# Scores in groups over six shared PSUM banks, in a fused block-sparse attention and MLP kernel

## The chip, the cores and the metric

The kernel runs on one core of a Trainium2 chip. The metric is device time in microseconds: the median of several executions. TensorE (PE) multiplies and writes its results to PSUM; VectorE (DVE) and ScalarE (ACT) read PSUM, compute and write to SBUF; GpSimd (POOL) issues most loads; SyncE (SP) issues transposing DMAs and stores. The engines run side by side, each its own instructions in order, and wait for each other by semaphores.

## The reference

```python
scores = (1/8) * q @ k.T                  # 4 batches, 8 heads, 768 tokens, 64 per head
mask   = |blk_i - blk_j| <= 1, first and last block row and column, and three sampled
         blocks for each of the 24 blocks of 32 tokens
attn   = softmax(where(mask, scores, -1e9))
x      = attn @ v                         # heads side by side: (4, 768, 512)
a1     = alpha1 * x + beta1
u      = x + lam * (w_tok @ a1)           # over tokens, w_tok 768 x 768
a2     = alpha2 * u + beta2
out    = u + lam * (relu(a2 @ w_ch1) @ w_ch2)     # 512 -> 2048 -> 512
```

## The kernel before

**The work.** Two heads of one batch are a pair; there are 16 pairs. The scores of a pair, keys on the partitions, are cut into 9 units of 1024 columns, 144 units in all. A unit goes through TensorE (scores), ScalarE (exponential, to a tile eT in f16), for pairs 6 to 15 VectorE (minimum with a mask tile, L760), and TensorE again (product with v). In pairs 0 to 5 ("single") the mask is folded into the score product by 24 more rows (88 rows, L651). In pairs 6 to 15 ("paired") the two heads lie on the two halves of the partitions, 64 rows each, and their score products run side by side in two row tiles of TensorE (L729). 90 units are paired ones.

**The lines that the text names.** On TensorE: L170 warming, L218 transposes of q and k, L228 the block mask, L651 and L729 scores, L691 and L787 products with v into the tile ops, L864 the token product, L946 the first channel product (four matmuls of 384 columns each, 128 times), L997 the second (groups of four matmuls of 512 columns into the tile cp or ops). On ScalarE: L666 and L755 exponentials, L959 relu of L946 into hts, L278 and L280 (VectorE) copies, among them that of the column b1t, which the first half of the first batch has beside each relu. On VectorE: L963 the same relu, L623 and L626 the normalisation of ops, L844 and L852 the input of the token product, L874 its sum into x_sb, L880 the input of the channel product, L456 scaling of w2b, L1014 the last sum ahead of a store (L1021). On SP: L590 transposes q and k of a paired pair, L911 transposes u. POOL loads at L316.

**The order.** It is not written out by hand. `Job` objects hold an engine, a length, a priority, dependencies and the buffers that they take and give. A loop at the end of the function plays the jobs by their lengths over the engines and emits each one when its engine is free, its inputs are there and its buffers can be had. `pin_order` then fixes this order on each engine. What the planner believes thus decides the order of instructions; the semaphores decide when they run.

**PSUM.** There are eight banks of 512 columns. Before, they are tiles of fixed kinds: two score buffers `sps` of two banks each, two buffers `mm` of one bank for transposes, token products and the first channel product, one `cp` and one `ops`. In `paired`, units are put in groups of two, and a group takes both `sps` at once:

```python
jq = Job("PE", 2 * 225.0 + 175.0, (1, i0), qk, deps, take=("sps", "sps"), give=give)
```

The 225 and 175 ns are the planner's lengths of a unit and of a visit to the scores. The channel product may take an `sps` only once no scores are left. `LEAD` (15 units) limits how far the scores of the later pairs may run ahead of the channel products. Each tile's dependencies are drawn by the framework, by tile.

Of the kernel before, what the change touches and what calls it, by code (L numbers as in the profile page):

```python
# [39 lines left out]
LEAD = 15  # L40
# [9 lines left out]
def pin_order(nc, tc):  # L50

    last = {}
    for ins in list(nc.cur_bb.bb.instructions):
        prev = last.get(ins.engine)
        if prev is not None:
            tc.add_manual_dep(
                ins,
                prev,
                mybir.DependencyInfo(
                    mybir.DependencyClass.NoSync, mybir.DependencyReason.DATA  # L60
                ),
                reason="program order",
            )
        last[ins.engine] = ins.name


@with_exitstack
def kernel(
# [78 lines left out]
    def mm_tile(shape, dt=FP):  # L147
        return ps.tile(shape, dt, name="mm", tag="mm", bufs=2)
# [66 lines left out]
    def transposes(rel, a, slots=range(NT)):  # L215
        tps = mm_tile([P, NT, P], BF)
        for o in slots:
            nc.tensor.transpose(tps[:, o, :], rel[:, a, o, :], identb[:])  # L218
        return tps[:].rearrange("p o c -> p (o c)")
# [3 lines left out]
    flatA = transposes(rel0, 0, range(0, 3))  # L223
    flatB = transposes(rel0, 0, range(3, 6))
    bqs = []
    for w, tag in ((0, "sps"), (1, "ops")):
        t = ps.tile([P, UN if tag == "sps" else 512], FP, name=tag, tag=tag, bufs=2 if tag == "sps" else 1)
        nc.tensor.matmul(  # L228
            t[0:NBLK, 0:HS], mbb[MB, :], kx[0][MB, ts(w, HS)], start=True, stop=True
        )  # L230
        bqs.append(t)
# [7 lines left out]
    for j in range(2, NQB):  # L239
# [14 lines left out]
        sps=2, mm=2, cp=1, ops=1, eT=NET, head=NQB, vext=NV, ld=NLD, rel=3,  # L254
# [5 lines left out]
    class Job:  # L260
        def __init__(self, eng, dur, prio, fn, deps=(), take=(), give=(), lat=None):
            self.eng = eng if isinstance(eng, tuple) else (eng,)
            self.dur, self.prio, self.fn = dur, prio, fn
            self.deps = list(deps)
            self.take, self.give = take, give
            self.lat = lat
            self.alt = {}
            self.xfer = None
            self.late = 0.0
            self.bulk = None  # L270
            self.done = None
            self.gate = None
            self.n = len(jobs)
            jobs.append(self)
# [146 lines left out]
    for t in range(NT):  # L421

        def tr(t=t):
            tl["wt", t] = tp = mm_tile([P, NT, P], BF)
            for s in range(NT):
                nc.tensor.transpose(tp[:, s, :], wtk_tile[0][:, t, s : S : NT], identb[:])

        def cp_(eng, t=t):
            copy(eng, wtokT[:, :, ts(t, P)], tl.pop(("wt", t))[:])

        j = Job("PE", mmt(NT, P), (5, t), tr, [wload["tok", t // 2]], take=("mm",))
        last = t == NT - 1
        wtok_jobs.append(
            Copy((4, t), cp_, [j], give=("mm", "w2b") if last else ("mm",), only=False)
        )
# [83 lines left out]
    for p in range(len(pairs)):  # L519
        if p == 0:  # L520
# [4 lines left out]
            def f_tr():  # L525
                tl["h0"] = transposes(rel0, 1)
# [9 lines left out]
            j = Job("PE", mmt(NT, P), (2, 0), f_tr, [j], take=("mm",))  # L536
            j = Copy((1, 0, 1), f_cq, [j, head_ready[0]], take=("head",), only=3 >= 0)
            j = Copy((1, 0, 2), f_ck, [j], give=("mm", "rel"), only=3 >= 0)
# [6 lines left out]
        elif p < NPE:  # L545
# [12 lines left out]
            for a in range(2):  # L558
                h = 2 * p + a

                def tr(p=p, a=a, h=h):
                    tl["hd", h] = transposes(rels[p], a)
# [7 lines left out]
                jt = Job("PE", mmt(NT, P), (2, p, a), tr, [ck, prev], take=("mm", "head"),  # L570
# [3 lines left out]
                prev = head_ready[h] = Job("NONE", 0.0, (0,), lambda: None, [j1, j2], give=("mm",), lat=0.0)  # L574
# [37 lines left out]
    grp = []  # L612
    exps = []
# [22 lines left out]
    def single(p):  # L636
# [3 lines left out]
        for u in range(NU):  # L640
            i = p * NU + u

            def qk(p=p, u=u):
                sps = ps.tile([P, UN], FP, name="sps", tag="sps", bufs=2)
# [29 lines left out]
            jq = Job("PE", mmt(2, 512) + (8 if u % 3 != 1 else 8), (1, i), qk, deps, take=("sps",), give=give)  # L674
            jq.gate = i
            qk_jobs[i] = jq
            exp_jobs[i] = je = Job("ACT", 950.0, (1, i), ex, [jq], take=("eT",), give=("sps",), lat=160.0)
# [35 lines left out]
    def paired(p):  # L713
        nonlocal last_pv
        b, n = pairs[p]
        mins = []
        for u in range(NU):
            i = p * NU + u
            grp.append((p, u))
            if len(grp) == 2:  # L720

                def qk(units_=tuple(grp)):
                    for pp_, u_ in units_:
                        sps = ps.tile([P, UN], FP, name="sps", tag="sps", bufs=2)
                        sl = slot_of(pp_)
                        for lo, jt, c, w in pieces(u_):
                            for a in range(2):
                                r = slice(a * D, (a + 1) * D)
                                nc.tensor.matmul(  # L729
                                    sps[:, a * 512 + lo : a * 512 + lo + w],  # L730
                                    kx[sl][r, ts(jt, P)],
                                    qx[sl][r, c : c + w],
                                    start=True,
                                    stop=True,
                                )
                        tl["sps", pp_, u_] = sps
                        st["qk"] += 1

                give = sum((("head",) for _, u_ in grp if u_ == NU - 1), ())
                deps = [head_ready[2 * pp_] for pp_, _ in grp]  # L740
                i0 = grp[0][0] * NU + grp[0][1]
                deps.append(qk_jobs[i0 - 1])
                jq = Job("PE", 2 * 225.0 + 175.0, (1, i0), qk, deps, take=("sps", "sps"), give=give)
                jq.gate = i
                for pp_, u_ in grp:
                    qk_jobs[pp_ * NU + u_] = jq
                grp.clear()

        for u in range(NU):
# [14 lines left out]
            exps.append((p, u, ex, mn))  # L764

        while exps and (exps[0][0] * NU + exps[0][1]) in qk_jobs:
            p_, u, ex, mn = exps.pop(0)
            i = p_ * NU + u
            je = Job("ACT", 950.0, (1, i), ex, [qk_jobs[i]], take=("eT",), give=("sps",), lat=160.0)
            min_jobs[i] = Job("DVE", 690.0, (1, i), mn, [je] + mask_jobs)  # L770
            if u == NU - 1:
                pv_of(p_)
# [55 lines left out]
    for p in range(len(pairs)):  # L828
# [29 lines left out]
        for g in range(2):  # L858

            def tok(p=p, g=g):  # L860
                tl["tp", p, g] = tp = mm_tile([P, 3, P])
# [10 lines left out]
            def xadd(p=p, g=g, n=n, s0=s0):  # L872
                sl = x_sb[:, s0 + 3 * g : s0 + 3 * g + 3, 2 * n * D : (2 * n + 2) * D]
                nc.vector.tensor_tensor(out=sl, in0=sl, in1=tl.pop(("tp", p, g))[:], op=ALU.add)  # L874
# [10 lines left out]
            jt = Job("PE", mmt(18, P), (3, p, g), tok, a_jobs + wtok_jobs, take=("mm",),  # L885
                     give=("a1p",) if g else ())
            jx = Job("DVE", 555.0, (1, p, g), xadd, [jt], give=("mm",))
# [8 lines left out]
        if b == 0:  # L896

            def utr(p=p):
                tl["up", p] = up = mm_tile([P, NT, P], BF)
# [3 lines left out]
            def ucp(eng, p=p, n=n, ut_tile=ut_tile):  # L903
                copy(eng, ut_tile()[:, n, 0:S], tl.pop(("up", p))[:].rearrange("p o c -> p (o c)"))

            j = Job("PE", mmt(NT, P), (2, p, 9), utr, ubs, take=("mm",), give=("ub",))
            ut_jobs[p] = Copy((1, p, 9), ucp, [j], take=take, give=("mm",))
# [22 lines left out]
    for kk in range(2 * B):  # L930
# [4 lines left out]
        for f in range(16):  # L935

            def c1(kk=kk, b=b, hf=hf, f=f, nc_=nc_):
                if f == 0:
                    hts[kk] = wk.tile([P, 16, HS], BF, name="hts", tag="hts", bufs=2)
                if tl.pop(("mmsel", kk, f)) == "sps":  # L940
                    hp = ps.tile([P, UN], FP, name="sps", tag="sps", bufs=2)
                else:
                    hp = mm_tile([P, 512])
# [31 lines left out]
            take = ((("mm", "sps"), ("mmsel", kk, f)),) + (("hts",) if f == 0 else ())  # L975
# [11 lines left out]
        for mi, (m, lo, w) in enumerate(parts):  # L987
            prev = last_m
            for r in range(4):

                def c2(kk=kk, m=m, r=r, mi=mi, lo=lo, w=w):
                    if r == 0:
                        tag = tl.pop(("cpsel", kk, mi))
                        shape = [P, UN] if tag == "sps" else [P, DM]
                        cps[kk, mi] = ps.tile(shape, FP, name=tag, tag=tag, bufs=2 if tag == "sps" else 1)
# [10 lines left out]
                take = ((("cp", "ops", "sps") if kk == 2 * B - 1 else ("cp", "ops"), ("cpsel", kk, mi)),) if r == 0 else ()  # L1006
# [33 lines left out]
    def can(j):  # L1040
        for t in j.take:
            if isinstance(t, tuple):
                opts = t[0]
                ok = False
                for o in opts:
                    if o == "sps" and not attention_over():
                        continue
# [4 lines left out]
                    if slots[o] > 0:  # L1052
# [9 lines left out]
    def gated(j):  # L1062
        return j.gate is not None and j.gate >= NS and j.gate - NS > st["ch"] / rate + LEAD

# [21 lines left out]
    while left:  # L1086
        moved = True
        while moved:
            moved = False
            for e in free_at:  # L1090
# [3 lines left out]
                if e == "POOL" and dma_free[0] - t > AHEAD:  # L1094
                    seq += 1
                    heapq.heappush(events, (dma_free[0] - AHEAD, -seq, None))
                    continue
                for r, j in by_eng[e]:
# [5 lines left out]
                    if (best is None or key < best[0]) and can(j):  # L1104
                        best = (key, j)
                if best is None:
# [3 lines left out]
                for tk in j.take:  # L1110
                    if isinstance(tk, tuple):
                        o = chosen[tk[1]]
                        slots[o] -= 1
# [31 lines left out]
                heapq.heappush(events, (j.done, seq, j))  # L1145
                if e == "PE":
# [9 lines left out]
                left -= 1  # L1156
# [6 lines left out]
        while events and events[0][0] <= t:  # L1163
# [7 lines left out]
            for g in j.give:  # L1171
                if isinstance(g, tuple):
                    slots[tl.pop(("slot", g))] += 1
                else:
                    slots[g] += 1
            for s in succ.get(j.n, ()):
# [3 lines left out]
                if not waiting[s.n]:  # L1180
                    for e in s.eng:
                        by_eng[e].append((t, s))
    pin_order(nc, tc)
# [30 lines left out]
```

## Time and profile before

| | us |
|---|---|
| median of 5 runs | 315.52 |
| lowest, highest | 315.1, 316.17 |
| the profiled execution, own time | 315.66 |
| its span, first to last instruction | 313.9 |
| busy: TensorE, VectorE, ScalarE | 305.5, 213.4, 198.1 |

The profile is of one execution. Busy time is the sum over an engine's instructions; the chain follows the work that ended last backwards, from each instruction to what released it. The timeline lists instructions by start. Ends of matmuls are modelled and overlap with the next start, so the pace of TensorE is read from start to start.

### The profile page before, as it was taken

How to read it: one execution, taken by the hardware profiler on the slowest of the kernel's cores; microseconds unless marked ns; L12 is line 12 of the kernel's file. 1: busy time of each engine (PE TensorE's matmuls, PEld its weight loads, DVE VectorE, ACT ScalarE, POOL GpSimd, SP SyncE). 2: the span in 40 equal slices, each digit the busy share in tenths (PEclk: the TensorE clock that was granted, in tenths of full speed). 3: DMA queues.
4: the chain of work that ended last, by engine and by line, in shares of the span. 5: the costliest groups of instructions: out<-in, count | busy, mean ns of one | idle time of the engine just before them, and what ended most of it. 6: DMA issues, size and time to landing. Idle time of an engine off the chain costs nothing.

```text
span 313.9 us, 7579 instructions
## 1 busy us (share of the span) xinstructions
PE 305.5 (97%) x3197; PEld 187.2 (60%) x3197; DVE 213.4 (68%) x447; ACT 198.1 (63%) x259; POOL 52.1 (17%) x91
## 2 busy tenths in 40 slices
PE   7999999988999999999999999999999999999995
PEld 3687888764646655565646655565656565555444
DVE  4599988859888687788869787788859671010111
ACT  4999988985778664766587654766587502828000
POOL 4646332000211220220310220230000000000000
PEclk9999999999999999999999999999999999999999
DMA  6999999994354555626462655626010203010021
GB/s 151 184 237 220 213 202 212 175 113 95 39 96 78 76 111 105 115 55 108 85 103 26 111 110 109 111 40 121 37 28 4 56 36 92 0 69 0 35 101 67
DMA packets 47210, 30.81 MB, mean 98 GB/s; under 512 B 27552, under 2 KB 43080, under 8 KB 47176
## 3 DMA queue, kind: packets, MB, share of 16 engines
q0 software_dynamic: 15984, 15.47, 31.9%
q1 hardware_dynamic: 30940, 14.61, 19.8%
q8 instruction: 25, 0.41, 0.7%
q10 hardware_dynamic: 252, 0.24, 0.3%
q14 instruction: 9, 0.07, 0.1%
HBM read 32.04 MB, written 6.33 MB: 122 GB/s over the span
## 4 chain that ended last, share of the span: by engine, by line
PE 80%; DMA 12%; issue 3%; DVE 2%; ACT 1%; POOL 1%; POOLq 0%
PE mm L946 23%; PE cp L997 22%; PE ops L787 8%; PE sps L729 7%; PE mm L864 7%; DMA v<-in_v_dram 6%; PE ops L997 5%; DMA k<-in_k_dram 4%; PE sps L946 2%; PE sps L651 2%; DMA q<-in_q_dram 2%; PE cp L170 2%; PE ops L691 1%; PE mm L218 1%; DVE ot L1014 1%
## 5 line engine op out<-in xcount | busy, mean ns | idle before, releaser
L755 ACT ACTIVATE eT<-sps 128x1024 f16<-128x1024 f32 x90 | 88.3, 1020 | 31.1 <-PE sps L729 28.8
L946 PE MATMUL mm<-uT,w1b 128*128 128x384 bf16 (+1 forms) x468 | 88.8, 326 | 2.7 <-DVE x_sb L874 2.2
L959 ACT ACTIVATE hts<-mm,b1t 128x384 bf16<-128x384 f32 x82 | 47.7, 582 | 49.3 <-PE mm L946 47.2
L997 PE MATMUL cp<-w2b,hts 128*128 128x512 bf16 (+1 forms) x320 | 76.9, 374 | 0.2
L946 PEld LDWEIGHTS <-w1b 128*128 128x128 bf16 x512 | 46.3, 97 | 34.7 <-issue 6.2
L760 DVE TENSOR_TENSOR eT<-eT,maskT 128x1024 f16<-128x1024 f16 x90 | 60.5, 684 | 4.1 <-ACT eT L755 4.0
L997 PEld LDWEIGHTS <-hts 128*128 128x128 bf16 x400 | 36.8, 97 | 35.7 <-issue 2.1
L666 ACT ACTIVATE eT<-sps 128x1024 f16<-128x1024 f32 (+1 forms) x55 | 52.1, 1024 | 3.1 <-PE sps L651 2.8
L787 PEld LDWEIGHTS <-eT 128*128 128x128 f16 x720 | 29.9, 97 | 15.9 <-issue 5.6
L1014 DVE TENSOR_TENSOR ot<-x_sb,cp 128x512 f32<-128x512 f32 (+1 forms) x20 | 13.4, 671 | 37.0 <-PE cp L997 36.8
L864 PE MATMUL mm<-a1p,wtokT 128*128 128x128 bf16 x576 | 36.2, 219 | 0.0
L787 PE MATMUL ops<-vext,eT 128*128 128x65 f16 x720 | 35.4, 193 | 0.0
L864 PEld LDWEIGHTS <-wtokT 128*128 128x128 bf16 x576 | 33.0, 98 | 2.1 <-issue 0.4
L651 PE MATMUL sps<-qx,kx 88*128 88x512 bf16 (+1 forms) x144 | 31.6, 325 | 0.6 <-ACT qx L237 0.5
L314 POOL COPY held<-flag 1x1 bf16<-1x1 bf16 x24 | 9.2, 384 | 130.7 <-DVE flag L334 130.7
L963 DVE TENSOR_SCALAR hts<-mm,b1t 128x384 bf16<-128x384 f32 x35 | 21.5, 616 | 13.5 <-PE mm L946 13.2
L729 PE MATMUL sps<-qx,kx 64*128 64x512 bf16 (+1 forms) x240 | 27.3, 326 | 0.0
L874 DVE TENSOR_TENSOR x_sb<-x_sb,mm 128x384 f32<-128x384 f32 x32 | 17.6, 550 | 4.7 <-PE mm L864 4.3
L691 PEld LDWEIGHTS <-eT 128*128 128x128 f16 x432 | 18.2, 97 | 4.4 <-DVE x_sb L626 0.6
L691 PE MATMUL ops<-vext,eT 128*128 128x65 f16 x432 | 20.2, 193 | 0.0
L626 DVE TENSOR_TENSOR x_sb<-ops,rcp 128x384 f32<-128x384 f32 x32 | 17.8, 557 | 1.1
L729 PEld LDWEIGHTS <-kx 64*128 64x128 bf16 x240 | 8.0, 94 | 16.5 <-issue 14.1
(71 smaller groups left out, 237.0 us busy)
## 6 DMA issues: line engine op xcount, KB each, us to landing
out_dram<-ot SPq DMA_DIRECT2D x23, 256.0 KB
v<-in_v_dram POOLq DMA_DIRECT2D x16, 192.0 KB, 5.5
q<-in_q_dram POOLq DMA_DIRECT2D x15, 192.0 KB, 4.1
k<-in_k_dram POOLq DMA_DIRECT2D x15, 192.0 KB, 4.4
w1b<-in_moe_w_ch_dram POOLq DMA_DIRECT2D x4, 512.0 KB, 9.9
w2b<-in_moe_w_ch_dram POOLq DMA_DIRECT2D x4, 512.0 KB, 15.9
wtk<-in_moe_w_tok_dram POOLq DMA_DIRECT2D x3, 384.0 KB, 9.5
maskT<-mask_rows SPq DMA_DIRECT2D x14, 72.0 KB
```

The costliest lines, as they stand in the source:

```text
L651: nc.tensor.matmul(sps[:, f - u * UN : f - u * UN + w], kx[h][0:KC, ts(jt, P)], qx[h][0:KC, c : c + w], start=True, stop=True,)
L666: nc.scalar.activation(eT[:, c], sps[:, c], AF.Exp, bias=EXPB, scale=SCALE)
L691: nc.tensor.matmul(ops[p, a][:, t * VW : t * VW + D + 1], eTs[p, u][:, ts(i - u * GU, P)], vx[:, a, jt, 0 : D + 1], start=(i % HT == 0), s ...
L729: nc.tensor.matmul(sps[:, a * 512 + lo : a * 512 + lo + w], kx[sl][r, ts(jt, P)], qx[sl][r, c : c + w], start=True, stop=True,)
L755: nc.scalar.activation(eT[:], sps[:], AF.Exp, bias=EXPB, scale=SCALE)
L760: nc.vector.tensor_tensor(out=e, in0=e, in1=maskT[:, u, :].unsqueeze(1).broadcast_to([P, 2, 512]), op=ALU.min,)
L787: nc.tensor.matmul(ops[p, a][:, t * VW : t * VW + D + 1], eTs[p, u][:, a * 512 + c * P : a * 512 + (c + 1) * P], vx[:, a, jt, 0 : D + 1], ...
L864: nc.tensor.matmul(tp[:, j, :], wtokT[:, s, ts(3 * g + j, P)], tl["a1p", p][:, s, :], start=(s == 0), stop=(s == NT - 1),)
L946: nc.tensor.matmul(hp[:, 0:nc_], w1b[:, dk, ts(f, P)], uTs[b][:, dk, hf * HS : hf * HS + nc_], start=(dk == 0), stop=(dk == 3),)
L959: nc.scalar.activation(hts[kk][:, f, :], hp[:, 0:HS], AF.Relu, bias=b1t[:, f : f + 1], scale=1.0)
L963: nc.vector.tensor_scalar(out=hts[kk][:, f, :], in0=hp[:, 0:HS], scalar1=b1t[:, f : f + 1], scalar2=0.0, op0=ALU.add, op1=ALU.max,)
L997: nc.tensor.matmul(cps[kk, mi][:, 0:w], hts[kk][:, nk, ts(m, P)], w2tile[0][:, nk, lo : lo + w], start=(nk == 0), stop=(nk == 15),)
```

## The change

The two `sps` and two `mm` buffers become one tile `ps6` of six banks, b0 to b5, in three pairs. Single products take one bank, scores two. While single-pair scores are left, they use b2 to b5 and single products b0 and b1, as before. Afterwards single products may take any bank, and do so first where the other bank of a pair is in use already. Scores of paired units are no longer jobs of their own: when TensorE is free the planner forms a group of two or three units from what is ready and from the free pairs (`heads_of_next`, `free_pairs`, `qk_group`). It holds back single products (`hold`) where a pair is missing and other work of at least `COVER` = 800 ns is at hand. `LEAD` becomes 18. Since all of it is one tile, `bank_order` draws the dependencies bank by bank, and adds those between instructions of different engines that share another tile by name.

```diff
-LEAD = 15
+LEAD = 18
+COVER = 800.0
+def bank_order(tc, instructions, psum, nb):
+    writer, readers = {}, {}
+    shared = {}
...
+        for b, kind in banks.items():
+            if kind == "outs":
+                for r in readers.get(b, ()):
+                    real[r.name] = r
+            elif b in writer:
+                real[writer[b].name] = writer[b]
+        real = {n: r for n, r in real.items() if r.engine != ins.engine}
+        for r in real.values():
+            tc.add_manual_dep(ins, r.name, sync, reason="bank")
+        for n in names:
+            for r in shared.get(n, ()):
+                if r.engine != ins.engine or ins.engine != mybir.EngineType.PE:
+                    real[r.name] = r
+            shared.setdefault(n, []).append(ins)
+        tc.declare_no_dep(ins, group=psum, keep=list(real.values()), reason="other banks")
...
-    def mm_tile(shape, dt=FP):
-        return ps.tile(shape, dt, name="mm", tag="mm", bufs=2)
+    ps6 = ps.tile([P, 6 * 512], FP, name="ps6", tag="ps6", bufs=1)
+    BANKS = tuple(f"b{i}" for i in range(6))
+    PAIRS = ("b0+b1", "b2+b3", "b4+b5")
...
-            jq = Job(..., (1, i), qk, deps, take=("sps",), give=give)
+            jq = Job(..., (1, i), qk, deps, take=((PAIRS[1:], ("spsb", p, u)),), give=give)
...
+    def heads_of_next(t):
+        i0 = st["qk"]
+        n = 0
+        while i0 + n < n_units and n < 3:
+            d = head_ready[2 * units[i0 + n][0]].done
+            if d is None or d > t:
+                break
+            n += 1
+        return n if n == 3 or n == n_units - i0 or n == 2 else 0
...
+        j = Job("PE", n * 225.0 + 175.0, (1, i0), qk, (), take=take, give=give)
...
-            take = ((("mm", "sps"), ("mmsel", kk, f)),) + (("hts",) if f == 0 else ())
+            take = ((BANKS, ("mmsel", kk, f)),) + (("hts",) if f == 0 else ())
...
+                if opts is BANKS:
+                    if hold[0]:
+                        return False
+                    opts = sorted(BANKS, key=lambda x: (not owned[other(x)], x))
+                    if st["qk"] < NPE * NU:
+                        opts = BANKS[:2]
+                    elif not hold[1] and any(owned.values()):
+                        opts = [x for x in BANKS if owned[x] or owned[other(x)]]
...
+                    n = heads_of_next(t)
+                    fp_ = free_pairs()
+                    m = min(n, len(fp_))
+                    later = n and gated(qk_group(n, []))
+                    hold[1] = not n or later
+                    hold[0] = n > m and not later and other_work(t) >= COVER
...
+                if n and m >= min(2, n) and (
+                    not best or not later and not hold[0] and best[0] > (False, (1, st["qk"]))
+                ):
+                    best = (None, qk_group(m, fp_))
...
+    bank_order(tc, list(nc.cur_bb.bb.instructions), ps6_name[0], len(BANKS))
     pin_order(nc, tc)
```

## Prediction

> **What bounds the kernel now.** I read the page from the top: busy time, the slices, the chain, and then the timeline of TensorE for the stage that the change touches.
>
> ```profile
> PE 305.5 (97%) x3197; PEld 187.2 (60%) x3197; DVE 213.4 (68%) x447; ACT 198.1 (63%) x259; POOL 52.1 (17%) x91
> PEclk9999999999999999999999999999999999999999
> PE 80%; DMA 12%; issue 3%; DVE 2%; ACT 1%; POOL 1%; POOLq 0%
> ```
>
> TensorE is busy for 97% of the span at full clock, and the chain that ended last runs over TensorE for 80% of it. No other engine passes 68%. So time is saved only by taking work off TensorE or by taking away a wait of TensorE. The 12% of DMA in the chain lie before 71 us: at 71.64 TensorE restarts after a wait of 2.19 us that goes back to the landing of a v tile, and everything after that is TensorE's own. The paired scores (L729) begin at 73.9 us.
>
> The busy figure can't show small waits, since ends of matmuls are modelled. I therefore go by starts. Lines of TensorE's timeline (start, duration, engine, line, operation, count):
>
> ```profile
> 103.76 1.03 PE L997 MATMUL cp<-w2b,hts 128*128 128x512 bf16 x4
> 104.62 1.46 PE L946 MATMUL mm<-uT,w1b 128*128 128x384 bf16 x8
> 106.02 0.61 PE L729 MATMUL sps<-qx,kx 64*128 64x256 bf16 x6
> 106.56 0.30 PE L787 MATMUL ops<-vext,eT 128*128 128x65 f16 x4
> ...
> 74.70 1.47 PE L946 MATMUL mm<-uT,w1b 128*128 128x385 bf16 x8
> 76.38 0.81 PE L946 MATMUL mm<-uT,w1b 128*128 128x385 bf16 x4 [0.21 <-ACT b1t L278]
> ...
> 83.71 1.72 PE L946 MATMUL mm<-uT,w1b 128*128 128x385 bf16 x8
> 85.27 1.03 PE L997 MATMUL cp<-w2b,hts 128*128 128x512 bf16 x4
> ...
> 87.02 1.47 PE L946 MATMUL mm<-uT,w1b 128*128 128x385 bf16 x8
> 88.74 0.82 PE L946 MATMUL mm<-uT,w1b 128*128 128x384 bf16 x4 [0.25 <-DVE b1t L280]
> ...
> 124.81 0.61 PE L729 MATMUL sps<-qx,kx 64*128 64x512 bf16 x4
> 125.53 1.02 PE L997 MATMUL cp<-w2b,hts 128*128 128x512 bf16 x4
> ```
>
> Two readings. First, the pace: four matmuls of 512 columns take 0.86 us from start to start, eight of 384 columns take 1.30 us where nothing waits. A group of two score units has 2 x 1024 columns, two heads side by side on 64 rows each, so 2 x 0.216 = 0.43 us of streaming. But from 106.02 to 106.56 it holds TensorE 0.54 us, and the eight L946 before it took 1.40 us instead of 1.30. So each visit to the scores costs 0.10 us on the way in and 0.11 us on the way out, 0.21 us that stream nothing. Second, the waits: 74.70 to 76.38 is 1.68 us where 1.30 would do, 83.71 to 85.27 is 0.26 us too long, 87.02 to 88.74 is 0.42 us too long, and 124.81 to 125.53 is 0.72 us where 0.54 is usual.
>
> Over all starts from 74 us to the end I find seven such places: 0.38, 0.26, 0.42, 0.18, 0.19 (194.92), 0.19 (250.63) and 0.09 us (251.68), together 1.71 us. Elsewhere TensorE has no gap.
>
> **The change part by part.** *Score groups.* The order of TensorE's instructions in the two programs differs only from the last single pair on, and the number of matmuls of every shape is the same. The 90 paired units are issued in 45 groups of two before, and in 38 groups after (24 of two, 14 of three). A third pair of banks is there, but loads, single products and the wish not to idle keep most groups at two. Seven visits fewer, at 0.21 us each: 1.47 us, all on the path.
>
> A rule of the skill gives another price. "TensorEngine Tiling (Array Packing)", Key Properties, says that changing the tiling mode drains TensorE; "TensorE: Matmul & The Clock Gate", Single matmul latency, puts the fixed part of a matmul at about 166 ns at full clock. A full drain in and out would be an estimated 0.33 us per visit, 2.3 us for seven. The rows show 0.21, so part of the drain overlaps; I take 1.47 and keep 2.3 for the range. Nothing in the rows allows less than about 1.3.
>
> *Waits of single products on banks.* Three of the seven waits are L946 on two mm buffers: three such products in a row (0.65 us each) must wait for the relu of the first. The need is 0.2 us from the last matmul to ScalarE's start, 0.16 for the b1t copy of the first half, 0.58 for the relu and about 0.06 for the semaphore, 1.0 us against 0.65 of cover. In the new order the products of that stretch stand apart (two, then a score group, then two with four L997 between) and later ones may take four or six banks. I added the trace's durations along VectorE's and ScalarE's queues in the new order: at the tightest place, the fourth product after the restart, VectorE has three w2b multiplies and a normalisation ahead, and its relu ends about 0.03 us after TensorE arrives. So 1.06 us go.
>
> *Waits of L997 on cp.* cp keeps its single bank. The L1014 add takes 0.68 us, with handovers 0.93. Before, only 0.75 us of TensorE work lay between two uses in two periods (hence 0.18 and 0.19); in the new order the least is 1.40. The two waits at 250 us lay behind a normalisation of ops (0.2 + 0.56 us) and a cp add; there the new order puts L946 products (1.30 us) ahead of the 36 L787. These four go too, 0.65 us. Together 1.71 us.
>
> *What is late next.* Banks are now shared, so scores wait for relus: 24 waits of score groups go to L959, 2 to L874 and 1 to L963, where before all went to exponentials; 18 waits of L946 go to exponentials. The cover is thin in places. In two score groups it is 0.86 us of TensorE work since the relu's product against a need of 0.84 plus what ScalarE still has in hand; I get 0.06 us late, twice. After groups of three the first L946 into the first unit's banks has 0.43 + 0.11 + 0.86 = 1.40 us of cover against 0.2 + 1.02 + 0.06 = 1.28 for the exponential. Sum of what I find late: 0.12 us.
>
> This is where a rule speaks against the change: the tiling page, PSUM Bottleneck, says that tiling speeds up TensorE but not the emptying of PSUM. A group of three puts three exponentials behind one burst of 0.85 us. Rows: two L755 in a row take 1.93 us, so three take 2.9, and a unit comes every (247 - 74) / 90 = 1.92 us in this stage. ScalarE needs 0.97 of that for the exponential and some 0.5 for relus. By the rule TensorE would have to wait for banks; by the rows it waits only where the next work also needs a bank, and L787 and L997 do not. I take the rows.
>
> *Semaphores.* With dependencies by bank, ScalarE's exponential waits for its own earlier exponential (long done, eleven units back) and takes TensorE's semaphore in a separate event instruction, where before the separate one was VectorE's, done early. ScalarE has 131 event instructions instead of 114, VectorE 63 instead of 53. The trace shows events of 51 ns at TensorE's queue; so an exponential starts some 0.05 us later once TensorE is done. ScalarE is not the bound; it counts at the roughly six places with under 0.15 us of spare: 0.3 us, between 0 and 0.8. Relus on ScalarE now also wait for VectorE's relu of the same hts tile 13 times, which the sums above contain. Twelve or so relus pass from VectorE to ScalarE (12 x 0.58 = 7 us, ScalarE at 65%), hidden.
>
> *The start.* Drawing by bank and tile name also ties the first copies: L232 now waits for the first block-mask product, L234 for ScalarE's L233, L235 for L232.
>
> ```profile
> 5.57 0.36 DVE L232 COPY kx<-mm 64x384 bf16<-64x384 bf16 x1 [0.38 <-PE mm L218]
> 5.78 0.45 PE L228 MATMUL sps<-kx,mbb 24*24 24x384 bf16 x1
> 6.34 0.55 DVE L236 CAST qx<-sps 24x384 bf16<-24x384 f32 x1
> 6.87 0.47 ACT L237 CAST qx<-ops 24x384 bf16<-24x384 f32 x1
> 7.39 1.03 PE L651 MATMUL sps<-qx,kx 88*128 88x512 bf16 x5 [0.50 <-ACT qx L237]
> ```
>
> L232 starts near 6.17, so L235 near 6.6 and L237 near 7.08 instead of 6.87; the first scores start 0.2 us later. It costs between 0 (the landing at 70.8 us decides the restart anyway) and 0.2; I take 0.2, since ScalarE is full there.
>
> *Moved without cost.* LEAD 18 lets scores run further ahead of the channel products: after the last L787 there are 156 L946 and 172 L997 instead of 128 and 176, work that moves behind the attention. From the last tokens product to the first L946 that needs its result there are 6.3 us of TensorE work (6.05 before), so the transpose of u stays hidden. POOL's order is unchanged; on SP transposes and stores change places, and those the scores need were at least as early as before. If that cover went, a late q or k would cost its 4 to 5.5 us landing.
>
> **Sum.** -1.47 - 1.71 + 0.12 + 0.3 + 0.2 = -2.56 us. The profiled execution took 315.66 us (span 313.9); that gives 313.1. The median is 0.14 below the profiled one, so 313.0.
>
> **Rivals.** *A, only the groups pay:* new small waits take the place of the seven old ones, at a like sum. -1.47 + 0.5 = -1.0, so 314.5. For it: 27 score waits on relus with thin cover. Against: the same way of adding, used on the old order, finds the old waits where the trace has them.
>
> *B, the shared banks couple TensorE to ScalarE, slower:* 45 places (27 scores on relus or adds, 18 products on exponentials) where TensorE would come late if the handover is longer than I think. Mean lateness of 0.06 us cancels the gain; at 0.1 us it is +4.5 - 2.6 = +1.9, 317.4. For it: the event ahead of each exponential, and relus queueing behind an exponential of 1.02 us. Against: most of these places have over 0.3 us of spare.
>
> *C, the gain turns into waiting for q and k:* faster scores meet tiles that arrive no sooner, 315.5. Against: one load chain ran from 95.9 to 109.9 us, 14 us, and the flag that starts it is raised some 16 units, 30 us, ahead of need.
>
> **How the numbers follow.** Main case 0.64 (312.0 to 314.0, with the bounds above), A 0.20 (313.7 to 315.2), C 0.06, B 0.10. About 0.2%, 0.63 us, is what can be told from no change here: faster means below 314.9. Main and most of A are faster: 0.78; the rest of A and most of C are the same: 0.11; B and a little of C slower: 0.11. Range 311.9 to 315.4: it leaves out B, part of C and the lowest part of the main case.
>
> **What would show it.** In the profile after: 240 paired score matmuls in 38 visits, with TensorE held about 0.75 us by a visit of three; no excess at the L946 after the restart nor at the L997 after the third score group of a period; the restart still near 71.6 us; first scores at 7.6. TensorE's wait for L959 ahead of scores would be the sign of B, excess of 0.1 us or more there in most periods. The prediction is wrong if visits of three cost more than 0.21 beyond their streaming, or if new waits sum to over 1 us.

## The result and the profile after

| | before | after |
|---|---|---|
| median, us (44 and 25 runs) | 315.58 | 311.61 |
| lowest, highest | 314.3, 318.73 | 310.72, 315.24 |
| ratio of after to before | | 0.9886 [0.9866, 0.9906] |
| the profiled execution, own time | 315.66 | 313.56 |
| its span | 313.9 | 311.8 |

The kernel is 1.1% faster, with a margin of 0.2% on either side. By the medians it gained 4.0 us. The forecast was 313.0 us, a gain of 2.56 us, with a range from 311.9 to 315.4 us. The measured ratio, applied to the 315.52 us of before, gives 311.9 us, the lower edge of that range, and the median of 311.61 us lies 0.3 us under it. The gain is larger than forecast, by one to one and a half us. It does not come from the granted TensorE clock: among executions that kept a mean of 0.998 or more, two sets of before have medians of 315.37 and 314.98 us, and two sets of after 311.36 and 311.59 us. The profiled execution of after lies 1.95 us above the median of its kernel, while that of before lies at its median; the two traces therefore show only 2.1 us of the gain, and the text below has to say where the rest is.

The page of after, busy times, clock and the chain's shares by engine, in the order in which the prediction showed them:

```profile
PE 303.0 (97%) x3197; PEld 188.9 (61%) x3197; DVE 207.1 (66%) x434; ACT 206.4 (66%) x272; POOL 52.9 (17%) x91
PEclk9999999999999999999999999999999999999999
PE 77%; DMA 16%; issue 2%; POOL 2%; DVE 1%; POOLq 0%
```

TensorE is still what bounds the kernel, at the same share of a shorter span. ScalarE has gained 13 instructions and 8 us of work, VectorE has 13 fewer and 6 us less; both have a third of the span free. The chain has more DMA in it, 16% instead of 12%. That is a first hint that the early loads, not the scores, make this execution longer than the median.

TensorE's timeline where the attention of the later pairs sets in, and at two visits to the scores (start, duration, engine, line, operation, count, and in brackets the idle time before and what ended it):

```profile
7.56 1.03 PE L716 MATMUL ps<-qx,kx 88*128 88x512 bf16 x5 [0.79 <-ACT qx L303]
...
70.62 0.83 PE L1026 MATMUL ps<-uT,w1b 128*128 128x385 bf16 x4 [1.60 <-DVE x_sb L957]
72.80 0.83 PE L1026 MATMUL ps<-uT,w1b 128*128 128x385 bf16 x4 [1.36 <-DVE x_sb L957]
73.56 0.61 PE L837 MATMUL ps<-qx,kx 64*128 64x512 bf16 x6
74.11 0.42 PE L756 MATMUL ops<-vext,eT 128*128 128x65 f16 x8
74.36 1.47 PE L1026 MATMUL ps<-uT,w1b 128*128 128x385 bf16 x8
75.67 1.03 PE L1076 MATMUL cp<-w2b,hts 128*128 128x512 bf16 x4
76.53 1.47 PE L1026 MATMUL ps<-uT,w1b 128*128 128x385 bf16 x8
77.93 0.61 PE L837 MATMUL ps<-qx,kx 64*128 64x512 bf16 x4
...
96.85 0.82 PE L837 MATMUL ps<-qx,kx 64*128 64x512 bf16 x8
97.61 0.54 PE L870 MATMUL ops<-vext,eT 128*128 128x65 f16 x12
...
106.53 0.82 PE L837 MATMUL ps<-qx,kx 64*128 64x512 bf16 x8
107.29 1.04 PE L1076 MATMUL cp<-w2b,hts 128*128 128x512 bf16 x4
```

The scores that were L729 are L837 here, the channel products L946 and L997 are L1026 and L1076, the relus L959 and L963 are L1039 and L1043, the exponential L755 is L789, the single-pair scores L651 are L716, and the sums L874 into x_sb are L957. A visit of three units holds TensorE from 96.85 to 97.61 us, 0.76 us, and again 0.76 us from 106.53. After 73.56 us no start is late: eight L1026 from 74.36 take 1.31 us, where before such a product had to wait for its relu just here (74.70 to 76.38). But the restart is at 72.80 us, later than the 71.64 us of before, and there are two waits ahead of it instead of one.

**The same sum for every kernel.** To compare orders that differ, I set each trace beside the program's own order of TensorE. From the start of the first paired score group to the start of the last run of second channel products, I add what the matmuls stream at the paces that the trace shows where nothing waits (0.216 us for 512 columns as in the prediction, and 0.162, 0.056 and 0.03 us for 384, 128 and 65), add 0.21 us for each visit to the scores (less 0.10, the way into the first, which lies ahead of the stretch), and call the rest waits. In the traces of the experiments the first matmul of that last run has no record: the step into it is 0.378 us where the two complete traces have 0.162. Its start is therefore taken 0.216 us ahead of the first one recorded.

| kernel | stretch, us | streaming | visits | waits |
|---|---|---|---|---|
| before | 216.43 | 205.15 | 45: 9.35 | 1.93 |
| after | 214.72 | 206.66 | 38: 7.88 | 0.18 |
| after, second execution | 215.53 | 206.66 | 38: 7.88 | 0.99 |
| groups of two, banks shared | 218.62 | 206.66 | 45: 9.35 | 2.61 |
| groups of two, banks divided | 219.52 | 206.66 | 45: 9.35 | 3.51 |
| LEAD 15 | 213.48 | 202.08 | 35: 7.25 | 4.15 |
| after, casts later | 214.71 | 206.66 | 38: 7.88 | 0.17 |
| before, casts later | 216.43 | 205.15 | 45: 9.35 | 1.93 |
| LEAD 16, casts last | 213.23 | 203.60 | 37: 7.67 | 1.96 |
| after, 52 more departures | 228.94 | 208.06 | 38: 7.88 | 13.00 |

The streaming differs because an order may put some work ahead of the first paired scores or behind them; it is not a gain or a loss. In the last row the waits hold the added departures, about 10.9 us, and about 1.7 us of a lowered clock. From before to after the visits fell by 1.47 us and the waits by 1.75 us. No single place of after is late by more than 0.06 us.

### The profile page after: what moved, and what is told of

It reads as the page before. It is cut to its first block, busy times and chain, and to the rows that moved or that the text cites. A ratio compares the mean times of both kernels' runs of the same rounds, so it can differ in the third digit from the quotient of the medians.

```text
span 311.8 us, 7605 instructions
## 1 busy us (share of the span) xinstructions
PE 303.0 (97%) x3197; PEld 188.9 (61%) x3197; DVE 207.1 (66%) x434; ACT 206.4 (66%) x272; POOL 52.9 (17%) x91
## 4 chain that ended last, share of the span: by engine, by line
PE 77%; DMA 16%; issue 2%; POOL 2%; DVE 1%; POOLq 0%
PE ps L1026 26%; PE cp L1076 22%; PE ops L870 8%; PE ps L837 8%; PE ps L947 7%; DMA v<-in_v_dram 6%; PE ops L1076 5%; DMA k<-in_k_dram 4%; DMA wtk<-in_moe_w_tok_dram 3%; DMA q<-in_q_dram 2%; DMA q2f<-in_q_dram 1%; POOL q L383 1%; POOL k L383 1%; POOL v L383 0%; DVE wtokT L347 0%
## 5 line engine op out<-in xcount | busy, mean ns | idle before, releaser
L789 ACT ACTIVATE eT<-ps 128x1024 f16<-128x1024 f32 x90 | 86.9, 1022 | 29.4 <-PE ps L837 28.6
L1026 PE MATMUL ps<-uT,w1b 128*128 128x384 bf16 (+1 forms) x512 | 93.0, 326 | 3.0 <-DVE x_sb L957 3.0
L1039 ACT ACTIVATE hts<-ps,b1t 128x384 bf16<-128x384 f32 x106 | 61.4, 582 | 40.4 <-PE ps L1026 36.5
L1076 PE MATMUL cp<-w2b,hts 128*128 128x512 bf16 (+1 forms) x320 | 77.2, 374 | 0.0
L794 DVE TENSOR_TENSOR eT<-eT,maskT 128x1024 f16<-128x1024 f16 x90 | 60.5, 685 | 12.5 <-ACT eT L789 12.2
L1026 PEld LDWEIGHTS <-w1b 128*128 128x128 bf16 x512 | 46.9, 98 | 33.3 <-DVE x_sb L957 3.5
L1076 PEld LDWEIGHTS <-hts 128*128 128x128 bf16 x400 | 36.6, 98 | 36.4 <-issue 3.0
L731 ACT ACTIVATE eT<-ps 128x1024 f16<-128x1024 f32 (+1 forms) x55 | 52.5, 1018 | 4.0 <-PE ps L716 3.8
L947 PE MATMUL ps<-a1p,wtokT 128*128 128x128 bf16 x576 | 36.2, 219 | 0.0
L716 PE MATMUL ps<-qx,kx 88*128 88x512 bf16 (+1 forms) x144 | 31.7, 326 | 0.8 <-ACT qx L303 0.8
L1093 DVE TENSOR_TENSOR ot<-x_sb,cp 128x512 f32<-128x512 f32 (+1 forms) x20 | 13.4, 672 | 28.4 <-PE cp L1076 28.3
L837 PE MATMUL ps<-qx,kx 64*128 64x512 bf16 (+1 forms) x240 | 26.1, 326 | 0.0
L957 DVE TENSOR_TENSOR x_sb<-x_sb,ps 128x384 f32<-128x384 f32 x32 | 17.6, 549 | 3.4 <-PE ps L947 3.1
L1093 DVE TENSOR_TENSOR ot<-x_sb,ops 128x512 f32<-128x512 f32 (+1 forms) x5 | 3.2, 635 | 22.5 <-PE ops L1076 22.5
L1043 DVE TENSOR_SCALAR hts<-ps,b1t 128x384 bf16<-128x384 f32 x22 | 13.6, 618 | 6.8 <-PE ps L1026 5.2
## 6 DMA issues: line engine op xcount, KB each, us to landing
w1b<-in_moe_w_ch_dram POOLq DMA_DIRECT2D x4, 512.0 KB, 10.9
```

Source lines behind the costliest of these rows:

```text
L716: nc.tensor.matmul(sps[:, f - u * UN : f - u * UN + w], kx[h][0:KC, ts(jt, P)], qx[h][0:KC, c : c + w], start=True, stop=True,)
L731: nc.scalar.activation(eT[:, c], sps[:, c], AF.Exp, bias=EXPB, scale=SCALE)
L789: nc.scalar.activation(eT[:], sps[:], AF.Exp, bias=EXPB, scale=SCALE)
L794: nc.vector.tensor_tensor(out=e, in0=e, in1=maskT[:, u, :].unsqueeze(1).broadcast_to([P, 2, 512]), op=ALU.min,)
L837: nc.tensor.matmul(sps[:, a * 512 + lo : a * 512 + lo + w], kx[sl][r, ts(jt, P)], qx[sl][r, c : c + w], start=True, stop=True,)
L947: nc.tensor.matmul(tp[:, j, :], wtokT[:, s, ts(3 * g + j, P)], tl["a1p", p][:, s, :], start=(s == 0), stop=(s == NT - 1),)
```

## The experiments

**After once more.** No edit; the kernel was run again beside the others, for its spread and for a second profile.

> The changed kernel once more, as the point of comparison for the others of this call. Its first profile restarted TensorE at 72.80 us, 1.2 us later than before (71.64), because the q tile landed late (its cast at 69.74 instead of 66.88 us); from the restart on it took 3.3 us less. Theory 1 (seven visits fewer at 0.21 us, and seven small waits gone, 1.71 us; early wait set by where loads land, different in each execution): about 3 us under before plus or minus what the landing does, 311.5 to 313. Rival (the gain comes also from an earlier restart): a profile whose restart lies ahead of 71 us and a time near 311.

Median 312.02 us (310.59 to 315.29), ratio 0.9873 [0.9835, 0.991]. The gain repeats. The profiled execution took 315.29 us, and its windows show why (stretch, length, busy us and counts of PE, PEld, DVE, ACT and POOL, granted TensorE clock, DMA share, GB/s):

```profile
66.00:70.00 4.00, 3.33 (x62) 2.82 (x59) 0.42 (x1) 3.12 (x4) 0.00 (x0) 1.00 0.75 112
70.00:74.00 4.00, 1.77 (x8) 0.73 (x8) 3.47 (x9) 0.74 (x2) 0.00 (x0) 0.86 1.31 169
74.00:78.00 4.00, 3.95 (x26) 1.88 (x26) 2.87 (x8) 2.71 (x6) 0.00 (x0) 0.72 0.25 50
```

TensorE is busy for 1.77 of 4 us from 70 us on, and over the following 4 us it is granted 0.72 of its clock. Its timeline there, to be read against the lines of after at 73.56 and 74.11 us:

```profile
70.89 0.83 PE L1026 MATMUL ps<-uT,w1b 128*128 128x385 bf16 x4 [1.56 <-DVE x_sb L957]
73.06 1.47 PE L1026 MATMUL ps<-uT,w1b 128*128 128x385 bf16 x4 [1.34 <-DVE x_sb L957]
74.45 1.04 PE L837 MATMUL ps<-qx,kx 64*128 64x512 bf16 x6
75.42 0.62 PE L756 MATMUL ops<-vext,eT 128*128 128x65 f16 x8
```

The L1026 at 73.06 us holds TensorE for 1.39 us instead of 0.76, the score group for 0.97 instead of 0.55. The first is 0.63 us too long and lies ahead of the stretch in the table; in the stretch the waits are 0.99 us instead of 0.18. Together this execution lost 1.4 us to the lower clock, which has nothing to do with banks or groups; the other 0.3 us that it is longer than the first is its later restart. So the stage ahead of the paired scores needed experiments of its own.

**Groups of two only.** Shared banks, bank-drawn dependencies and LEAD 18 stay; only the third unit goes.

```diff
-        while i0 + n < n_units and n < 3:
+        while i0 + n < n_units and n < 2:
...
-        return n if n == 3 or n == n_units - i0 or n == 2 else 0
+        return n if n == 2 or n == n_units - i0 else 0
```

> The changed kernel with groups of at most two units: 45 visits to the scores instead of 38, banks shared as in the change. If visits cost 0.21 us each, it is 1.5 us slower than the changed kernel, near 313 to 313.5, and its small waits stay gone. If the gain came from groups of three alone, it is back at before, 315.5. If from the sharing of banks alone, it equals the changed kernel.

317.24 us (315.41 to 319.77), ratio 1.0057 [1.0029, 1.0084]: slower than before by half a per cent. The expectation missed by 4 us. There are 45 visits again, as expected, but the waits are back too, 2.61 us of them at other places. The largest:

```profile
118.67 0.81 PE L1076 MATMUL cp<-w2b,hts 128*128 128x512 bf16 x3
119.31 0.29 PE L870 MATMUL ops<-vext,eT 128*128 128x65 f16 x4
120.25 2.75 PE L1076 MATMUL cp<-w2b,hts 128*128 128x512 bf16 x12 [0.65 <-DVE ot L1093]
```

The second channel product at 120.25 us waits for the add that empties cp (L1093). That is the kind of wait that the prediction listed under L997, and cp is the same single bank in all versions. So sharing six banks does not by itself take away the waits. Whether they are there depends on the order that the planner makes. Visits and waits explain 3.9 us of the distance to after (218.62 against 214.72 us). Half of its 14 runs had a lowered granted clock, against 8 of the 25 of after, and that accounts for part of the rest.

**Groups of two, banks divided as before.** On top of the last edit, paired scores get only the two upper pairs of banks, and single products only b0 and b1 until the attention is over.

```diff
-        return [x for x in PAIRS if slots[x[:2]] and slots[x[3:]]]
+        return [x for x in PAIRS[1:] if slots[x[:2]] and slots[x[3:]]]
...
-                    if st["qk"] < NPE * NU:
+                    if not attention_over():
                         opts = BANKS[:2]
```

> The changed kernel with PSUM divided as before (single products b0 and b1, scores b2 to b5 until no scores are left) and groups of at most two, dependencies still drawn by bank. 45 visits, as with groups of two over shared banks, which took 317.24 us and had 2.8 us of waits after the first paired scores. If sharing the banks is what makes waits, this has fewer: I count 1.7 us of them from the durations, so about 1 us less than that one, near 315.5, equal to before. If sharing is what removes waits, it is slower than that one, 318 or more.

316.28 us (314.36 to 318.14), ratio 1.0005 [0.9973, 1.0038]: the kernel before, within what can be told. What remains of the change here is the drawing of dependencies by bank, the groups formed at issue, and LEAD 18. Together they give no measurable gain and no measurable cost. Of the 3.51 us of waits in its profiled execution about 1.2 fall between 73 and 77 us, where this execution too had a lowered clock (0.62 between 74 and 78 us), so that figure is not one of the order alone. The same groups with shared banks were 1 us slower by the medians; the two intervals overlap, so sharing showed no gain there, and a loss is not settled.

**LEAD back to 15.** Groups of three, shared banks, and the old limit on how far scores run ahead.

```diff
-LEAD = 18
+LEAD = 15
```

> The changed kernel with LEAD back at 15. Its order has 35 visits (20 of three, 15 of two) instead of 38. By the price of a visit it is 0.6 us faster than the changed kernel if no new waits come; if the further lead of 18 units is what keeps TensorE free of waits, it is slower by some waits of 0.2 us, 1 us or more.

316.13 us (315.1 to 318.94), ratio 1.0017 [0.9995, 1.0039]: no gain is left. It has the fewest visits, 35 with 20 groups of three, worth 2.1 us against before. Yet it waits for 4.15 us. TensorE's timeline at the first such place:

```profile
76.79 0.81 PE L1076 MATMUL cp<-w2b,hts 128*128 128x512 bf16 x3
78.00 0.82 PE L837 MATMUL ps<-qx,kx 64*128 64x512 bf16 x8 [0.40 <-DVE hts L1043]
79.51 0.83 PE L1026 MATMUL ps<-uT,w1b 128*128 128x385 bf16 x4 [0.69 <-ACT eT L789]
```

A score group waits 0.40 us for a relu that holds its bank, and right behind it a channel product waits 0.69 us for an exponential that holds its own. Both are the mechanism of rival B, coupling through shared banks, and it comes once more, when a token product waits 0.75 us for an exponential at 207.59 us. It is real; the order at LEAD 18 avoids it, this one does not. It is not all of the 4.15 us, though. Second channel products wait for the add that empties cp, as before the change (0.22 us at 126.33 us), and two more wait 0.30 and 0.31 us, at 135.39 and 196.21 us.

**The price of a departure.** Between the units of a group TensorE is made to leave the two-row-tile mode for one short product of full height, whose result the unit then overwrites.

```diff
                 sps = two_banks(banks[k_])
                 sl = slot_of(p)
+                if k_:
+                    nc.tensor.matmul(sps[:, 0:64], warm[:, 0:P], warm[:, 0:64], start=True, stop=True)
```

> The changed kernel with one full-height product of 64 columns (result overwritten) ahead of the second and third unit of each group: 52 more departures from the scores' row tiles, everything else in its order. It prices a departure by itself. At 0.21 us and 0.03 for the product: 52 x 0.24 = 12.5 us, 324. By a full drain in and out, 0.33: 52 x 0.36 = 18.7 us, 330. If a visit cost little and the gain came from elsewhere: 52 x 0.03 = 1.6 us, 313.

324.81 us (322.58 to 327.06), ratio 1.0265 [1.0192, 1.0339]. The order of the rest is that of after. One visit of three in the timeline:

```profile
97.88 0.39 PE L839 MATMUL ps<-qx,kx 64*128 64x512 bf16 x2
98.20 0.20 PE L835 MATMUL ps<-warm 128*128 128x64 bf16 x1
98.34 0.39 PE L839 MATMUL ps<-qx,kx 64*128 64x256 bf16 x4
98.66 0.20 PE L835 MATMUL ps<-warm 128*128 128x64 bf16 x1
98.80 0.39 PE L839 MATMUL ps<-qx,kx 64*128 64x512 bf16 x2
99.12 0.54 PE L872 MATMUL ops<-vext,eT 128*128 128x65 f16 x12
```

From 97.88 to 99.12 us is 1.24 us where after takes 0.76: 0.24 us for each of two departures, of which 0.03 stream the 64 columns (64 x 0.216 / 512). So 0.21 us for leaving and coming back, the price that the prediction read from the pace of before. There are 52 departures more; 52 x 0.24 = 12.5 us, and the median rose by 13.2. Two of the four runs had a lowered granted clock; compared with the runs of after at a like clock, the rise is 11.9 and 12.2 us, 0.23 us for each departure.

**The casts of pair 7 later, on after.** Ahead of the restart, VectorE stands behind loads. Its timeline in after (the releaser in brackets):

```profile
69.74 0.36 DVE L571 COPY rel<-q 128x768 bf16<-128x768 bf16 x1 [3.62 <-DMA q<-in_q_dram]
70.02 0.55 DVE L957 TENSOR_TENSOR x_sb<-x_sb,ps 128x384 f32<-128x384 f32 x1
70.73 0.36 DVE L571 COPY rel<-k 128x768 bf16<-128x768 bf16 x1 [0.17 <-DMA k<-in_k_dram]
71.00 0.55 DVE L963 TENSOR_TENSOR ub<-x_sb,a_bc 128x384 bf16<-128x384 f32 x1
71.92 0.36 DVE L892 COPY vext<-v 128x768 f16<-128x768 f16 x1 [0.37 <-DMA v<-in_v_dram]
72.20 0.55 DVE L957 TENSOR_TENSOR x_sb<-x_sb,ps 128x384 f32<-128x384 f32 x1
```

The sum of the token product into x_sb (L957) is what TensorE's restart needs, and it stands in VectorE's order behind the cast of a q tile (L571) that landed late; TensorE's two waits go back to these two L957. The edit raises the landing time that the planner believes for the loads of this pair by 2 us, so that it emits the first sum ahead of the q cast and the second ahead of the k cast. It changes VectorE's order only around these lines, and no other engine's.

```diff
-            ld[p, nm].late = 1500.0 if hold_ else 0.0
+            ld[p, nm].late = 1500.0 if hold_ else 2000.0 if p == NPE + 1 else 0.0
```

> The changed kernel with one belief of the planner changed: q, k and v of the eighth pair count as landed 2 us later. TensorE's, ScalarE's and the queues' orders are the same; on VectorE the two sums of the token product (L957) stand ahead of, or between, the casts that wait for these loads instead of behind them. If the wait at 69 to 73 us is only VectorE standing in front of a late load, TensorE restarts at about 69 us, and 2 to 3 us are gained: 308.5 to 309.5. If what follows needs the late tiles at once, the wait only moves, and the time stays within 0.5 us of the changed kernel.

310.97 us (310.66 to 314.71), ratio 0.9873 [0.9832, 0.9915]. TensorE's timeline there now has one wait in place of two, and the paired scores begin 2.9 us earlier than in the profiled execution of after:

```profile
68.23 1.47 PE L1026 MATMUL ps<-uT,w1b 128*128 128x385 bf16 x8
70.70 0.61 PE L837 MATMUL ps<-qx,kx 64*128 64x512 bf16 x6 [1.00 <-DMA kx<-rel]
```

Part of the 2.9 us is where the loads landed. In the experiment with more departures, whose order up to here is that of after, they landed early and the paired scores began at 71.47 us, 0.8 us later than here. The median is 0.6 to 1.0 us below that of after, within the spread of both. So neither of the two expectations was met, a gain of 2 to 3 us or none beyond 0.5; the profiles show the wait moving, the times alone do not prove a gain.

**The same edit on the kernel before.** This separates what the change is worth from the wait ahead of it.

> The kernel before with the one belief changed that also helped the changed kernel (q, k and v of the eighth pair land 2 us later), so that VectorE does the first sum of the token product ahead of the casts. If the early wait is common to both kernels and independent of the change, it gains what it gained there, 0.7 to 2.5 us: 313 to 315. If the wait only moves in the old order, 315.5.

313.6 us (313.3 to 314.31), ratio 0.9921 [0.9895, 0.9948]. The old wait of 2.19 us at the restart is gone, and 0.51 us remain for the landing of kx:

```profile
69.29 1.47 PE L946 MATMUL mm<-uT,w1b 128*128 128x385 bf16 x8
70.60 1.03 PE L997 MATMUL cp<-w2b,hts 128*128 128x512 bf16 x3
72.14 0.61 PE L729 MATMUL sps<-qx,kx 64*128 64x512 bf16 x6 [0.51 <-DMA kx<-rel]
```

The seven old small waits are still there (1.93 us, as in before). With the edit in both, the change takes the median from 313.6 to 310.97, 2.6 us. The two were run beside different runs of before (medians 315.58 and 315.61), and the two ratios, 0.9873 and 0.9921, differ by 1.5 us with an uncertainty of about as much. So this pair agrees with the predicted 2.56 us but doesn't narrow it down; the sums of the traces do that better.

**LEAD 16 and the casts last.** A search for a version without either fault: the same line with 2700 in place of 2000, and LEAD 16.

> The changed kernel with LEAD 16 and the eighth pair's loads believed 2.7 us later, so that VectorE does both sums of the token product ahead of all three casts. 37 visits; from the durations I count 1.0 us of waits after the first paired scores, where the changed kernel has none. Theory (the early wait is VectorE standing before a load): no wait near 69 to 73 us, which gains another 1.1 us over the variant with the casts between the sums (310.97), less 0.2 for a visit, plus 1.0 of waits: 310.5 to 311.5. If the tiles are needed at once, 312.

311.1 us (310.7 to 311.7), ratio 0.9842 [0.9805, 0.9879], the narrowest spread of all. TensorE does not wait at the restart at all:

```profile
68.29 1.47 PE L1026 MATMUL ps<-uT,w1b 128*128 128x385 bf16 x8
69.60 0.41 PE L756 MATMUL ops<-vext,eT 128*128 128x65 f16 x8
69.84 2.12 PE L1026 MATMUL ps<-uT,w1b 128*128 128x385 bf16 x12
71.80 1.03 PE L1076 MATMUL cp<-w2b,hts 128*128 128x512 bf16 x3
72.76 0.61 PE L837 MATMUL ps<-qx,kx 64*128 64x512 bf16 x6
```

It pays 1.96 us of small waits later on, where 1.0 was expected, so what it wins early it gives back in part. It and the version with LEAD 18 and later casts beat before beyond doubt; against after they are 0.5 to 1 us better by the medians, which these runs can't settle.

## Why the prediction was right, and where it was off

*Seven visits fewer, -1.47 us: right.* 45 visits became 38, a visit of three takes 0.76 us (0.75 was said), and the experiment with 52 more departures gives 0.21 us each. The Trainium skill, "TensorEngine Tiling (Array Packing)", Key Properties, says that a change of mode drains TensorE. That agrees in kind. By an estimate from the skill's "TensorE: Matmul & The Clock Gate", Single matmul latency, the full fixed part of a matmul in and out is 0.33 us. The 52 departures would then have cost 52 x 0.36 = 19 us; they cost 12 to 13.

*Seven waits gone, -1.71 us: right.* The waits fell from 1.93 to 0.18 us. The experiments add that this belongs to one order, not to the shared banks as such: with groups of two, or with LEAD 15, the banks are shared just as well and the waits are 2.61 and 4.15 us. The prediction followed the order instruction by instruction, so it did not need that distinction, but its title for the step ("later ones may take four or six banks") gives the banks more credit than they earn.

*New waits +0.12 and semaphores +0.3: wrong, both near nothing.* All that is left is 0.18 us, where before had 0.22 beside the seven named, and no place is late by more than 0.06 us. The 17 further event instructions of ScalarE find cover everywhere. Their price was misread as well. The prediction took 51 ns from events at TensorE's queue, but ScalarE's event instructions ahead of exponentials take 17 ns, in the trace of before (74 of them at L755) and of after (71 at L789). These two terms are the mis-sized ones; leaving them out gives 312.5 for the median instead of 313.0 (the sum becomes -2.98 us), and the 0.3 is the larger error.

*The start, +0.2: right in size, not on the path.* The first scores start at 7.56 instead of 7.39 us, but after waits 2.96 us for loads later on, so a start 0.17 us earlier would have gone into those waits.

*"The restart still near 71.6 us": wrong in this execution.* It came at 72.80, because the q cast waited until 69.74 us. Both sums behind loads (L957) then came late; before, the q cast ran at 66.88 us, the first sum at 67.15 was in time, and only the second was late. The work from the restart on is the same in both kernels. From the restart to the start of the last run of matmuls before needed 308.49 - 71.64 = 236.85 us and after 306.43 - 72.80 = 233.63: 3.22 us less, against the 3.18 that visits and old waits were said to bring, or 2.76 with the two mis-sized terms. The later restart gives 1.16 back, and 315.66 - 3.22 + 1.16 = 313.6 is the profiled 313.56.

*The median is another 0.75 us better than the 3.22.* The same order, in the experiment with more departures, restarted at 70.70 us, 0.94 earlier than before, with a single wait of 1.96 us, because its q tile landed in time for the cast at 67.03. An execution like that would take 315.66 - 3.22 - 0.94 = 311.5 us, which is where the median is. That the median execution of after is of this kind was not seen in a profile of one, so it is argued and not shown. Five profiled executions have this order of VectorE there, and they fall in two kinds. With the q cast at 67.03 and 67.08 us (more departures, groups of two) TensorE restarts at 70.70 and 70.74; with it at 69.00 to 70.01 us (divided banks and both of after) it restarts at 72.57 to 73.06. Why loads land at such different times in executions of one order stays open. The prediction held the restart fixed. If this reading holds, about 0.75 us of the gain came without being foreseen, by luck and not by the mechanism.

*The rivals.* A fell for this order: the new waits are 0.18 us, not a sum like the old one. B did not decide, but its mechanism is part of what made LEAD 15 lose its gain, and what the skill's tiling page warns of under PSUM Bottleneck shows there as 0.69 and 0.75 us behind exponentials. C fell: no score group of after waits for q or k once the paired scores have begun.

## What to carry to other kernels

Read a stall or a mode's price from start to start in the trace, and then follow the new order instruction by instruction: fewer visits alone were worth nothing with LEAD 15 (35 visits, 4.15 us of waits), and more banks alone were worth nothing with groups of two. When a planner decides the order, a resource that it may use more freely is not a gain in itself; what counts is whether each wait finds work ahead of it. And before a small edit is sized, look at where the profiled execution lies in its runs: a q tile that was ready 2.7 us later (its cast at 69.74 instead of 67.03 us) went with a restart 2.1 us later, half the gain.

## What the runs showed of the hardware

After waits in the stage ahead of the paired scores the granted TensorE clock sometimes fell, well inside the kernel. Three profiled executions show it at half for 3.41 us. They are the second one of after, groups of two with divided banks, and after with more departures, in this order (windows as above):

```profile
72.87:76.28 3.41, 3.22 (x20) 1.40 (x21) 2.60 (x6) 1.66 (x3) 0.00 (x0) 0.50 0.70 145
73.63:77.04 3.41, 3.19 (x21) 1.52 (x19) 3.03 (x6) 2.51 (x5) 0.00 (x0) 0.50 0.29 58
72.51:75.92 3.41, 3.19 (x16) 1.48 (x13) 2.19 (x6) 2.40 (x4) 0.00 (x0) 0.50 0.29 58
```

The waits ahead of these were 1.56 and 1.34 us, 1.64 and 1.85 us, and in the third a single long one of 1.96 us. TensorE was not idle: in the 3.41 us just ahead of each drop it was busy for 0.83, 1.55 and 1.80 us. The first execution of after had waits of 1.60 and 1.36 us at the same place and kept its clock, although it too was busy for only 0.83 us from 69.02 to 72.43 us:

```profile
70.00:74.00 4.00, 2.02 (x14) 0.83 (x14) 3.46 (x9) 1.04 (x4) 0.00 (x0) 1.00 1.21 172
74.00:78.00 4.00, 4.00 (x34) 2.18 (x32) 3.93 (x9) 3.48 (x7) 0.00 (x0) 1.00 0.25 49
```

So the waits allow the drop but don't force it. The Trainium skill, "TensorE: Matmul & The Clock Gate", Part 1, says that the clock is taken back after an idle window of about 3.4 us, and that this window runs freely. The 3.41 us that each drop lasted agree with that length, and a free-running window would explain why equal waits are punished in one execution and not in another; no run here tests that. "Idle" has to be read loosely here, with TensorE busy for up to 1.80 of the 3.41 us.

In the three versions with later casts TensorE was busy for at least 2.4 us in any 3.41 us between 64 and 80 us, and the clock in their profiles was 1.00 there. Only 1 of their 22 runs had a mean granted clock below 0.998, against 11 of the 36 runs of after and 18 of 61 of before. Of the 25 runs of after in the result, the 8 with such a clock have a median of 314.2 us, the others 311.4. A wait of TensorE can thus cost more than its own length: 1.4 us more in the second execution of after. That the rest of those 2.8 us is the late restart itself is likely, but not shown.
